# Local and global attention with token routing: global queries scheduled one step earlier, and token ranks from half of the comparisons

## The chip, the cores and the metric

The kernel runs on one core of a Trainium2 chip. A core has five engines, each working through its own queue of instructions in order: PE (TensorE, the matrix unit, whose weight loads are shown as PEld), DVE (VectorE), ACT (ScalarE), POOL (GpSimd) and SP (SyncE, which only issues transfers here). Data lies in the on-chip memory SBUF; matmuls write to the small accumulation memory PSUM, which PE can't read. The engines wait for one another with semaphores.

The metric is device microseconds for one execution. Lower is better.

## The reference

There are 8 batches and 8 heads of width 64, 512 local tokens and 32 global ones.

```python
s_g = scale * q_g @ concat(k_g, k_l).T          # global queries see every key
out_g = softmax(s_g) @ concat(v_g, v_l)
s_ll = scale * q_l @ k_l.T, masked to |i - j| <= 32
s_lg = scale * q_l @ k_g.T                      # local queries see a window and the global keys
out_l = softmax(concat(s_lg, s_ll)) @ concat(v_g, v_l)
x = concat(out_g, out_l) as [8, 544, 512]
scores = x @ w_gate
for b in range(8):                              # the 128 tokens of the highest score
    top = argpartition(-scores[b], 128)[:128]
    y = relu(x[b, top] @ w1) @ w2               # w1 is 512 x 1024, w2 is 1024 x 512
    out[b, top] = x[b, top] + sigmoid(scores[b, top]) * y
```

So every batch needs its attention first, then a choice of 128 of its 544 tokens, then two dense layers on these, which are called the expert work below.

## The kernel before

**Steps.** The attention is cut into 32 steps, the list `work`: for each batch `b`, for each group `hq` of four heads, for each half `hf` of the local tokens. Two steps share one group's queries, keys and values. A group n covers steps 2n and 2n+1. The main loop is a pipeline over three steps. In step i it

- transposes the probabilities of step i (`transp`, L216) into a PSUM tile,
- computes the scores of step i+2 (`scores`, L188) and adds the mask and takes the row maxima on DVE (`maxima`, L201 and L203),
- takes the exponentials of step i+1 on ACT (`exps`, L209, eight instructions),
- copies the transposed tile to SBUF on ACT (`turned`, L221),
- multiplies the probabilities of step i-1 with the values (`attend_mm`, L238) and normalizes them on DVE (`attend_out`, L249 to L256).

**Global queries.** They use the same keys and values of the group. For group n, `g_scores` (L284), the maximum `g_max` (L288) and the exponential `g_exp` (L298) are at the end of step 2n, `g_transp` (L311) and the copy `g_turned` (L316) at the end of step 2n+1, and `g_attend` (L326) and `g_out` (L336 to L345) in step 2n+2. `g_out` stores the result to memory, and for a batch's second group reads all 32 rows back as tile `xg` for their scores.

**PSUM.** `s_tile()` hands out a pool of two buffers (tiles named s_ps). Each step takes three: the transposes, the scores, and the tile `big` of the global queries. The output of attend has one buffer (o_ps), taken anew in each step; the columns behind the local results hold the global result and a small tile of the ranking. The expert work takes its tiles from a third pool of two (m_ps).

**Loads.** `load` fetches q_t, k_t and qg_t of a group, with two buffers each, `load_v` one half of its values, with four buffers. `load` for group n+2 stands at the head of step 2n+1; both halves of the values of group n+1 are asked for in step 2n, behind `g_out`. SP issues all of these and the stores of `finish` and `g_out`. The order on PE, DVE, ACT and POOL is that of the program text (`manual_schedule`, L70); the order on SP is set by a planner.

**Ranks.** When a batch is complete, its tokens' scores are on DVE (`score`, L269, one fused multiply and sum per 128 tokens). Then a generator `chain` takes it through stages, one per step: score of the global rows, `spread` (all 544 scores laid along the free axis of every partition, tile r), `rank` for the five blocks of tokens, `onehot`, `gather`, and a wait of two steps. `rank(b, i)` compares every token of block i with all tokens: one instruction counts those of greater or equal score up to and including its own block (L371), one those of greater score from its own block on (L373); the matrix side_w holds the weights 0 and 1 that break ties by position. A token's rank is the sum of both. `onehot` (L381, L383) compares the ranks with the slot numbers 0 to 127, `gather` turns that into a list of token numbers by five matmuls of one column (L398) and fetches the rows with an indirect transfer (L403). The list `RATE` says how many blocks are ranked per step.

**Expert work.** It is cut into pieces in a list `fill`, each with a cost (1.3 for twelve matmuls of L485 or six of L501), and `run_fill` puts a third of a step's share at three places of each step; the share is at most `FILL` and is worked out from what is left and when it is due. Batches are taken in `GROUPS`. `work` items that are not done by the last step follow it, with the last batch's ranking between them: `GPRE`, `TAKES` and `GPOS` say how many pieces stand ahead of it, behind each block's ranking, and behind the onehot. Functions put into the list `early` run in the next step between attend_mm and attend_out.

## Time and profile before

| | |
|---|---|
| median of three runs | 366.64 us |
| the three runs | 366.64, 362.34, 366.88 us |
| the profiled execution | 365.06 us |
| its span, from first to last instruction | 363.3 us |
| mean granted TensorE clock | 0.921 |
| busy share of PE, DVE, ACT, POOL | 78, 68, 45, 10 % |
| bytes moved | 76.07 MB |

The profile was taken in one execution. Its page gives the busy time of each engine over the span. The trace behind it can be cut into windows (busy time of each engine in each), grouped by source line (busy time, mean duration, and the idle time of the engine ahead of the group), listed by waits (engine, line, what released it: us in total, how often, the longest), followed back from the end as a chain of waits, or read as a timeline. A name such as L188 is the line of the kernel that recorded the instruction; "s_ps<-k_t,q_t" says that it writes tile s_ps and reads k_t and q_t. A wait on "issue" ends on nothing that the profile shows. Matmuls overlap, so a busy PE is not a PE at its peak.

### The profile page before, as it was taken

Reading aid. Unit: us, or ns where it says so; the run is one execution under the profiler, and the core shown is the slowest. Engines: PE = TensorE matmul, PEld = TensorE weight load, DVE = VectorE, ACT = ScalarE, POOL = GpSimd, SP = SyncE. Lnnn points to the kernel's source line nnn. Section 1 sums busy time; section 2 is a strip of 40 time slices with the busy share of each in tenths; the row PEclk is TensorE's granted clock in tenths of the full one; section 3 lists DMA queues with packets and bytes.
Section 4 is the critical chain, followed back from the end, with each engine's and each line's share of the span. In section 5 each row is a group of like instructions: output and inputs, shape, how many; then the busy total and the mean of one; then the engine's idle time right before and its main releaser. Section 6 shows DMA issues by size and latency. Waiting matters only on the chain.

```text
span 363.3 us, 13847 instructions
## 1 busy us (share of the span) xinstructions
PE 283.6 (78%) x6136; PEld 225.8 (62%) x6136; DVE 245.4 (68%) x593; ACT 164.0 (45%) x411; POOL 37.9 (10%) x30
## 2 busy tenths in 40 slices
PE   6768484865496978878779699889788982989994
PEld 3546363654374766756567688667568871779883
DVE  1466555569977896799769867996678769293222
ACT  1644919091738264837454357235644620112020
POOL 1000505040230001001000100010000101111111
PEclk9989969698859899999969999999999996799998
DMA  7995979697849486875867648496770122101000
GB/s 257 416 387 190 346 276 324 220 359 257 278 127 383 165 308 203 320 279 183 284 231 231 241 161 316 135 329 202 287 286 20 23 74 69 39 20 59 31 29 29
DMA packets 22636, 76.07 MB, mean 209 GB/s; under 512 B 6576, under 2 KB 7984, under 8 KB 18480
## 3 DMA queue, kind: packets, MB, share of 16 engines
q1 hardware_dynamic: 21296, 70.99, 54.3%
q0 software_dynamic: 1280, 4.20, 3.6%
q8 instruction: 48, 0.79, 0.9%
q14 instruction: 12, 0.10, 0.1%
HBM read 64.16 MB, written 11.01 MB: 207 GB/s over the span
## 4 chain that ended last, share of the span: by engine, by line
issue 61%; PE 13%; DMA 7%; DVE 7%; POOL 4%; ACT 4%; SPq 1%; POOLq 1%; ACTq 0%; DVEq 0%
DMA k_t<-in_kT_dram 5%; PE s_ps L188 5%; PE o_ps L238 3%; POOL xe L403 2%; POOL out_dram L508 2%; PE o_ps L326 2%; ACT p_t L209 1%; DVE nb L203 1%; DVE p_t L201 1%; DMA qg_t<-in_qgT_dram 1%; PE s_ps L216 1%; DVE x L256 1%; DVE mx L288 1%; ACT pg L298 1%; PE m_ps L457 1%
## 5 line engine op out<-in xcount | busy, mean ns | idle before, releaser
L209 ACT ACTIVATE p_t<-p_t,nb 128x128 f32<-128x128 f32 x256 | 78.2, 394 | 13.0 <-DVE nb L203 8.6
L188 PE MATMUL s_ps<-k_t,q_t 64*32 64x128 f32 x2048 | 44.9, 308 | 37.7 <-ACT pg L298 18.5
L201 DVE SCALAR_TENSOR_TENSOR p_t<-s_ps,cs 128x1024 f32<-128x1024 f32 x32 | 39.1, 1223 | 49.0 <-PE s_ps L188 49.0
L188 PEld LDWEIGHTS s_ps<-k_t,q_t 64*32 64x32 f32 x2048 | 33.6, 117 | 46.7 <-ACT pg L298 21.7
L238 PE MATMUL o_ps<-v_t,pt 128*32 128x65 f32 x2048 | 42.8, 238 | 6.5 <-issue 6.5
L238 PEld LDWEIGHTS o_ps<-v_t,pt 128*32 128x32 f32 x2048 | 36.0, 120 | 15.3 <-issue 13.5
L298 ACT ACTIVATE pg<-s_ps,nbg 128x64 f32<-128x64 f32 (+1 forms) x32 | 13.8, 483 | 69.4 <-DVE nbg L290 57.9
L203 DVE TENSOR_REDUCE nb<-p_t 128x8 f32<-128x1024 f32 x32 | 39.0, 1220 | 1.1
L216 PE MATMUL s_ps<-cs,p_t 128*128 128x128 f32 x256 | 37.1, 291 | 2.9 <-ACT pt L221 1.5
L216 PEld LDWEIGHTS s_ps<-cs,p_t 128*128 128x128 f32 x256 | 30.8, 148 | 6.1 <-ACT pt L221 1.9
L221 ACT COPY pt<-s_ps 128x1024 f32<-128x1024 f32 x32 | 31.9, 996 | 0.5 <-PE s_ps L216 0.5
L371 DVE SCALAR_TENSOR_TENSOR junk<-r,sc,side_w 128x128 f32<-128x128 f32 (+4 forms) x40 | 23.8, 595 | 3.1 <-ACT r L359 1.7
L485 PE MATMUL m_ps<-xTh,w1h 128*128 128x256 f32 x84 | 22.5, 301 | 4.1 <-DVE hTl L488 3.2
L403 POOL DMA_INDIRECT xe<-out_dram,ix x8 | 9.0, 1120 | 152.8 <-DVE ix L401 119.3
L501 PE MATMUL m_ps<-w2h,hTh 128*128 128x512 f32 x56 | 24.9, 444 | 0.0
L269 DVE CUSTOM_DVE_ANT_0 junk<-x,wgb 128x512 f32<-128x512 f32 x32 | 24.2, 757 | 0.8
L373 DVE SCALAR_TENSOR_TENSOR junk<-r,sc,side_w 128x544 f32<-128x544 f32 (+4 forms) x40 | 22.6, 565 | 1.6
L501 PE MATMUL m_ps<-w2l,hTh 128*128 128x512 f32 x56 | 23.1, 412 | 0.0
L256 DVE TENSOR_TENSOR x<-o_ps,rec 128x512 f32<-128x512 f32 x32 | 22.1, 692 | 1.1
L485 PE MATMUL m_ps<-xTh,w1l 128*128 128x256 f32 x84 | 20.7, 279 | 0.0
L284 PE MATMUL s_ps<-k_t,qg_t 64*32 64x512 f32 (+1 forms) x256 | 20.5, 438 | 0.0
L316 ACT COPY ptg<-s_ps 128x768 f32<-128x768 f32 x16 | 12.8, 800 | 14.8 <-PE s_ps L311 14.7
(113 smaller groups left out, 424.8 us busy)
## 6 DMA issues: line engine op xcount, KB each, us to landing
v_t<-in_vw_dram SPq DMA_DIRECT2D x32, 1040.0 KB, 5.9
k_t<-in_kT_dram SPq DMA_DIRECT2D x15, 832.0 KB, 7.9
out_dram<-x SPq DMA_DIRECT2D x32, 256.0 KB, 5.1
q_t<-in_qT_dram SPq DMA_DIRECT2D x15, 512.0 KB, 7.4
ws<-in_w_dram SPq DMA_DIRECT2D x8, 512.0 KB, 7.6
q_t<-in_qT_dram SPq DMA_DIRECT2D x2, 256.0 KB
qg_t<-in_qgT_dram SPq DMA_DIRECT2D x16, 32.0 KB, 5.9
out_dram<-ogs SPq DMA_DIRECT2D x16, 32.0 KB
```

The source lines that it names most:

```text
L188: nc.tensor.matmul(out=s_ps[32 * j:32 * j + 32, par, pr, t, :], lhsT=q_t[rows, pr, 32 * c:32 * c + 32], rhs=window(k_t[rows, pr, k0:k0 + P ...
L201: nc.vector.scalar_tensor_tensor(out=p_t, in0=s_ps.rearrange("p a r t k -> p (a r) t k"), scalar=0.125, in1=m, op0=ALU.mult, op1=ALU.add)
L203: nc.vector.tensor_reduce(out=nb, in_=p_t.rearrange("p q t k -> p (q t) k"), axis=AX.X, op=ALU.max, negate=True)
L209: nc.scalar.activation(out=p_t[:, q, t, :], in_=p_t[:, q, t, :], func=AF.Exp, bias=nb[:, 2 * q + t:2 * q + t + 1])
L216: nc.tensor.transpose(t_ps[:, t, q, :], p_t[:, q, t, :], ident)
L221: nc.scalar.copy(out=pt, in_=t_ps)
L238: nc.tensor.matmul(out=o_ps[32 * j:32 * j + 32, t, h, :], lhsT=pt[:, t, 2 * (h % 2) + h // 2, 32 * j:32 * j + 32], rhs=v_t[:, 4 * t + j, h ...
L256: nc.vector.tensor_tensor(out=xt[b, hf][:, :, 4 * hq:4 * hq + 4, :], in0=o_ps[:, :, :, 0:D], in1=rec.broadcast_to([P, 2, 4, D]), op=ALU.mult)
L269: nc.vector.tensor_tensor_reduce(out=junk[:n, 0:DM], in0=xf, in1=wgb[:n], op0=ALU.mult, op1=ALU.add, scale=1.0, scalar=0.0, accum_out=dst,)
L371: nc.vector.scalar_tensor_tensor(out=junk[:n, 0:hi], in0=r[:n, 0:hi], scalar=s, in1=side_w[:n, P + SL - lo:P + SL - lo + hi], op0=ALU.is_g ...
L485: nc.tensor.matmul(out=h_ps, lhsT=a[:, kc, ms], rhs=xT[x_][:, kc, :], start=(i == 0), stop=(i == len(prods) - 1))
L501: nc.tensor.matmul(out=y_ps, lhsT=hT[h_][:, mc, cc], rhs=w[:, mc, :], start=(part == 0 and i == 0), stop=(part == 3 and i == len(prods) - 1))
```

## The change

- The global queries go one step earlier: `g_scores`, `g_max` and `g_exp` of group n+1 in step 2n+1 (the first group's ahead of the loop), `g_transp` and `g_turned` of group n in step 2n, `g_attend` and `g_out` of group n in step 2n+1. Their tile is filled right behind the scores of step i+2, ahead of the first third of the expert pieces, and is emptied on ACT behind that third.
- `turned` stands ahead of the masks and maxima and of the exponentials.
- `load` of group n+2 stands at the head of step 2n. The values of group n+1 are asked for at the heads of steps 2n and 2n+1, one half each.
- A batch's `chain` begins one step earlier; all five blocks are ranked in one step, and `RATE` is gone.
- Block i is compared only with the tokens from its own block on. The outcomes are kept, as ones and zeros in fp16 (`won`). The sum along a row is the number of later tokens that beat a token, as before. For the earlier tokens, `beaten` lets PE sum the outcomes by column against a column of minus ones, 15 matmuls per batch into the o_ps bank; what is missing to a count of the earlier tokens that win is a constant per token, and it is put into the slot numbers that `onehot` compares with, `slot16`, now one row set per block.
- Some constants and scratch tiles become smaller, the last ranking's takes change.

```diff
-RATE = (3, 2.5, 3, 2.5, 3, 2.5, 3)
-TAKES = (1, 1, 1, 1, 1)
-GPOS = 3
+TAKES = (1, 0, 1, 0, 0)
+GPOS = 1
...
-    side_w = cst.tile([P, SL + 2 * P], FP32, name="side_w")
-    nc.gpsimd.memset(side_w[:, P:P + SL], 1.0)
+    side_w = cst.tile([P, ST], FP16, name="side_w")
+    nc.gpsimd.memset(side_w[:, P:ST], 1.0)
+
+    won = [cst.tile([P, P * (NT + 1 - i)], FP16, name=f"won{i}") for i in range(NT + 1)]
+    for i in range(NT + 1):
+        nc.gpsimd.memset(won[i][:, ST - P * i:], 0.0)
+    nc.gpsimd.memset(won[NT], 0.0)
+    neg1 = cst.tile([P, 1], FP16, name="neg1")
+    nc.vector.memset(neg1, -1.0)
...
-    slot16 = cst.tile([P, NST * P], FP16, name="slot16")
+    slot16 = cst.tile([P, NT + 1, NST * P], FP16, name="slot16")
...
-        junk = moe.tile([P, ST], FP32, name="junk")
+        junk = moe.tile([P, DM], BF16, name="junk")
...
     def rank(b, i):
         r, cnt = rk[b]
         n = P if i < NT else SG
-        s = sc[b][0:n, i:i + 1]
-        lo, hi = P * i, P * i + n
-        junk = moe.tile([P, ST], FP32, name="junk")
-        nc.vector.scalar_tensor_tensor(out=junk[:n, 0:hi], in0=r[:n, 0:hi], scalar=s, in1=side_w[:n, P + SL - lo:P + SL - lo + hi],
-                                       op0=ALU.is_ge, op1=ALU.mult, accum_out=cnt[:n, i, 0:1])
-        nc.vector.scalar_tensor_tensor(out=junk[:n, lo:ST], in0=r[:n, lo:ST], scalar=s, in1=side_w[:n, 0:ST - lo],
-                                       op0=ALU.is_gt, op1=ALU.mult, accum_out=cnt[:n, i, 1:2])
+        lo = P * i
+        nc.vector.scalar_tensor_tensor(
+            out=won[i][:n, 0:ST - lo], in0=r[:n, lo:ST], scalar=sc[b][0:n, i:i + 1], in1=side_w[:n, 0:ST - lo],
+            op0=ALU.is_gt, op1=ALU.mult, accum_out=cnt[:n, i:i + 1])
+
+    def beaten(b):
+        ps = ob["o"][:, 0, 4 * VD + SG:4 * VD + SG + NT + 1]
+        for a in range(NT + 1):
+            for i in range(a + 1):
+                n = P if i < NT else SG
+                nc.tensor.matmul(out=ps[:, a:a + 1], lhsT=won[i][0:n, P * (a - i):P * (a - i) + P], rhs=neg1[0:n],
+                                 start=(i == 0), stop=(i == a), skip_group_check=True)
+        rk[b] = (ps, rk[b][1])
...
     def onehot(b):
-        _, cnt = rk[b]
+        ps, cnt = rk[b]
         rank_t = sm.tile([P, NT + 1], FP16, name="rank")
-        nc.vector.tensor_tensor(out=rank_t, in0=cnt[:, :, 0], in1=cnt[:, :, 1], op=ALU.add)
+        nc.vector.tensor_tensor(out=rank_t, in0=ps, in1=cnt, op=ALU.add)
...
-            out=oh[b], in0=slot16.rearrange("p (a n) -> p a n", a=1).broadcast_to([P, NT + 1, NST * P]),
+            out=oh[b], in0=slot16,
...
-        i = 0
-        acc = 0.0
-        while i <= NT:
...
-        if RATE[b] <= 2:
-            yield
+        for i in range(NT + 1):
+            rank(b, i)
+        early.append((beaten, (b,)))
+        yield
         onehot(b)
...
     load(0, 0)
+    load(0, 1)
     load_v(0, 0, 0)
-    load(0, 1)
     load_v(0, 0, 1)
...
-        nc.sync.dma_start(out=side_w[:, 0:P], in_=const[:, o:o + P])
-        nc.sync.dma_start(out=side_w[:, P + SL:], in_=const[:, o + P:o + 2 * P])
+        tri = wst.tile([P, 1024], FP32, name="ws")
+        nc.sync.dma_start(out=tri[:, 0:P], in_=const[:, o:o + P])
+        nc.gpsimd.tensor_copy(out=side_w[:, 0:P], in_=tri[:, 0:P])
...
     exps(*PR[0])
+    big = s_tile()
+    g_scores(0, 0, big)
+    gst["pg"] = g_exp(big, g_max(big))
     for i in range(nstep + 1):
...
-            if hf == 1 and i // 2 + 2 < B * NQ:
-                load(*divmod(i // 2 + 2, NQ))
+            if hf == 0 and n + 2 < B * NQ:
+                load(*divmod(n + 2, NQ))
+            if n + 1 < B * NQ:
+                load_v(*divmod(n + 1, NQ), hf)
...
         if i + 2 < nstep:
-            PR[i + 2] = maxima(work[i + 2], scores(work[i + 2]))
+            s_ps = scores(work[i + 2])
+        if g is not None:
+            PT[i] = turned(t_ps)
+        if i + 2 < nstep:
+            PR[i + 2] = maxima(work[i + 2], s_ps)
         if i + 1 < nstep:
             exps(*PR[i + 1])
+
+        big = nb = None
+        if g is not None and (hf == 0 or n + 1 < B * NQ):
+            big = s_tile()
+            if hf == 0:
+                g_transp(gst["pg"], big)
+            else:
+                g_scores(*divmod(n + 1, NQ), big)
+                nb = g_max(big)
         if g is not None:
-            PT[i] = turned(t_ps)
             run_fill(part / 3)
+        if big is not None:
+            if hf == 0:
+                gst["ptg"] = g_turned(big)
+            else:
+                gst["pg"] = g_exp(big, nb)
         if i > 0:
             o_ps = attend_mm(work[i - 1], PT.pop(i - 1))
-            if i % 2 == 0:
+            if i % 2:
                 g_attend(*work[i - 1][:2], gst["ptg"])
...
-            if i % 2 == 0:
+            if i % 2:
                 g_out(*work[i - 1][:2])
-
-        if g is not None and hf == 0 and nxt[0] < B:
-            for k in range(2):
-                load_v(*nxt, k)
         if g is not None:
             run_fill(part / 3)
-            big = s_tile()
-            if hf == 0:
-                g_scores(b, hq, big)
-                gst["pg"] = g_exp(big, g_max(big))
-            else:
-                g_transp(gst["pg"], big)
-                gst["ptg"] = g_turned(big)
...
-        if 1 < i < nstep and i // per_b and i % per_b == 1:
+        if 1 < i < nstep and i // per_b and i % per_b == 0:
             chains.append(chain(i // per_b - 1))
...
-            nc.vector.tensor_copy(out=slot16, in_=slot)
+            for a in range(NT + 1):
+                nc.vector.tensor_scalar(out=slot16[:, a], in0=slot, scalar1=tokid[:, a:a + 1],
+                                        scalar2=float(SG if a < NT else -SL), op0=ALU.subtract, op1=ALU.add)
...
         rank(B - 1, i)
         take(TAKES[i])
+    beaten(B - 1)
     onehot(B - 1)
```

18 lines of the change are left out of this document (5 added, 13 removed).

## The prediction

> **What bounds the kernel now.** I read the engine totals of the page first.
>
> ```profile
> span 363.3 us, 13847 instructions
> PE 283.6 (78%) x6136; PEld 225.8 (62%) x6136; DVE 245.4 (68%) x593; ACT 164.0 (45%) x411; POOL 37.9 (10%) x30
> ```
>
> No engine is full over the span, so the limit has to be read by stage. The next view cuts the span at the first local transpose of a step (step 0 at 11.3, step 9 at 88.2, step 31 at 288.6); its columns are busy time of PE, PEld, DVE, ACT, POOL, then PE's granted clock, the DMA share and GB/s.
>
> ```profile
> 11.30:88.20 76.90, 52.05 (x1462) 39.48 (x1462) 45.43 (x87) 43.87 (x108) 14.45 (x6) 0.87 0.84 304
> 88.20:160.00 71.80, 56.29 (x1453) 43.33 (x1445) 58.49 (x135) 38.47 (x95) 7.22 (x4) 0.90 0.72 255
> 160.00:226.00 66.00, 53.74 (x1313) 44.47 (x1311) 52.09 (x130) 35.82 (x95) 3.32 (x3) 0.95 0.69 244
> 226.00:288.60 62.60, 53.96 (x1294) 43.53 (x1293) 50.98 (x131) 31.21 (x82) 3.32 (x4) 0.97 0.53 186
> 288.60:306.80 18.20, 9.71 (x227) 8.56 (x225) 13.13 (x44) 3.87 (x8) 0.59 (x1) 0.88 0.24 80
> 306.80:363.30 56.50, 50.31 (x269) 42.27 (x269) 21.98 (x66) 8.84 (x23) 7.80 (x7) 0.92 0.09 33
> ```
>
> Three stages: nine early steps without expert work (8.5 us each, PE busy two thirds), 22 steps with it (200.4 us, PE busy 164.0, the sum of three rows), and a tail of 74.7 us. The same view cut by head groups (two steps each) shows a second pattern.
>
> ```profile
> 78.13:99.61 21.48, 11.17 (x350) 8.63 (x348) 20.34 (x45) 11.94 (x27) 4.71 (x2) 0.88 0.80 274
> 134.69:151.21 16.52, 13.82 (x365) 10.58 (x364) 11.31 (x25) 9.18 (x24) 1.15 (x1) 1.00 0.80 286
> 151.21:168.99 17.78, 14.32 (x372) 11.15 (x370) 17.04 (x45) 9.61 (x24) 0.00 (x0) 1.00 0.77 267
> ```
>
> A group in which a batch is ranked has DVE full (20.34 of 21.48, 17.04 of 17.78); a group without ranks has DVE at 11.31 of 16.52. So one group of each batch is bound by DVE, the other by what PE waits for. Those waits, for steps 9 to 31, then for the early steps:
>
> ```profile
> PE s_ps L188 <- ACT pg L298: 12.9, 8, 3.5
> PE s_ps L311 <- ACT pt L221: 4.3, 4, 2.0
> PE s_ps L188 <- DMA k_t<-in_kT_dram: 3.5, 3, 2.2
> ...
> PE s_ps L188 <- DMA k_t<-in_kT_dram: 5.6, 2, 4.4
> PE s_ps L188 <- ACT pg L298: 5.5, 4, 1.8
> PE s_ps L188 <- issue: 4.8, 2, 2.8
> ```
>
> The chain of waits shows how the early steps are tied together:
>
> ```profile
> 51.25 2.02 PE s_ps L284 x16
> ...
> 55.24 1.16 PE s_ps L188 x64
> ...
> 57.16 7.56 DMA k_t<-in_kT_dram
> 64.86 1.96 PE s_ps L188 x64
> ```
>
> k_t has two buffers. The global scores (L284) are the last reader of one, ending at 53.3; only then may the keys two groups ahead be fetched, and the fetch goes out at 57.16 and takes 7.56 us, while the scores that need it (L188) stand next on PE. That loop closes once per group.
>
> **The change, part by part.** The sum is made against the profiled execution, 365.06 us (span 363.3 plus 1.8 around it); the median of the three runs, 366.64, lies 1.6 above it.
>
> *Global queries one step ahead.* g_scores of group n moves from step 2n to step 2n-1, right behind the local scores; g_transp to 2n, g_attend and g_out to 2n+1. The last read of k_t then comes a step earlier, and `load` moves from the head of the odd step to that of the even one, so the 7.56 us have about two steps more, some 17 us. The k_t waits go: 5.6 and 3.5. The two v_t loads are split over two steps; both value halves still have over a step. On SP the loads now stand at other places among the stores of finish, the ogs store and the xg read, which waits for that store; SP's order is not fixed by the program text but by the planner (rival 1).
>
> The global tile sits in the same two-buffer pool as the scores. Today it is emptied at the end of a step, and the next L188 waits for the exp (L298): 5.5 and 12.9 us. Now it is emptied in mid-step, behind which a third of the filling, attend and two more thirds follow on PE, so I let both numbers go. In exchange PE meets the global tile right behind L188 and needs the local copy `turned` (L221) done; everything else of the step is queued behind that wait. The change puts the copy ahead of the eight exps on ACT, where it stood behind them, and L188 covers it:
>
> ```profile
> L221 ACT COPY pt<-s_ps x32: 984/995/1014, 15.6 to 289.8; 128x1024 f32<-128x1024 f32 x32
> L371 DVE SCALAR_TENSOR_TENSOR junk<-r,sc,side_w 128x128 f32<-128x128 f32 (+4 forms) x40 | 23.8, 595 | 3.1 <-ACT r L359 1.7
> L371 DVE DVE_READ_ACCUMULATOR junk<-r,sc,side_w 128x1 f32 x32 | 2.7, 83 | 0.0
> L373 DVE SCALAR_TENSOR_TENSOR junk<-r,sc,side_w 128x544 f32<-128x544 f32 (+4 forms) x40 | 22.6, 565 | 1.6
> L398 PEld LDWEIGHTS <-oh x40: 90/96/116, 98.5 to 326.9; 128*128 128x128 f16 x32, 32*128 32x128 f16 x8
> 306.81 0.38 PE L398 MATMUL s_ps<-tok,oh 128*128 128x1 f16 x5 [8.50 <-DVE oh L383]
> ```
>
> 0.995 us against the 1.16 of L188: nothing is left to wait, and the L311 wait on that copy (4.3) goes too. Without this cover the copy would cost up to 1 us per step (rival 3).
>
> *Half the comparisons.* L371 goes, with its accumulator reads: (23.8 + 2.7) / 8 = 3.3 us of DVE per batch; the five of L373 stay, 22.6 / 8 = 2.8 and five reads of 0.08. Their output becomes fp16 while one input stays fp32; I expect the duration of now (bounds: 0 to half less). In the ranked groups this takes DVE from 17.04 to 13.7 of 17.78, so DVE no longer stands in the way when PE's waits go: without it the gain from the global shift would end at DVE's 17.
>
> *Counting on PE.* `beaten` adds 15 matmuls of one column per batch. Nearest row: five of the same shape in L398 take 0.38. Three times that is 1.1, and the pipeline's fill counts once instead of three times, so I take 0.9, by the row of the same shape in sequence; upper bound 15 loads of 0.096 end to end, 1.4; lower 0.7. The Trainium skill, "TensorE: Matmul & The Clock Gate", section "LDWEIGHTS (loading the stationary operand)", speaks against the change: a load costs its columns, here 128, at 1.2 GHz, an estimate of 107 ns and 1.6 us per batch. By it the sum would be some 5 us higher over eight batches; the trace's five in 0.38 do not agree with it. `beaten` is queued ahead of attend_out, so DVE's den waits 0.9 longer in one step of four, where DVE has room now. It writes into the o_ps bank, of which there is one: the next attend waits for the onehot's read in the step before; that read stands a third of a step ahead of it on DVE, so I cost it at nothing, and at about 1.5 us (two scores, L269 below) once per batch if DVE lags.
>
> *Order of the chain.* Each batch's chain starts one step earlier and ranks in one step. By the program's credits (costs 1.3 per piece), 9.1 units are left after the steps before and 6.5 after: two ffn2 pieces leave the tail.
>
> *Small things.* Three const loads become two, slot16 is written by five small operations instead of one, POOL gets some memsets and a copy: DVE has 31 us free in the early stage and POOL is 10% busy, so nothing; uncovered they cost 1 to 2 us once.
>
> Rows for the sums, of the expert matmuls just after the tail's gap and when warm, of DVE's groups, and of the gather's transfer (us to landing):
>
> ```profile
> 307.71 0.63 PE L501 MATMUL m_ps<-w2l,hTh 128*128 128x512 f32 x1
> 308.14 0.63 PE L501 MATMUL m_ps<-w2h,hTh 128*128 128x512 f32 x1
> ...
> 313.94 0.40 PE L501 MATMUL m_ps<-w2h,hTh 128*128 128x512 f32 x1
> 314.17 0.39 PE L501 MATMUL m_ps<-w2l,hTh 128*128 128x512 f32 x1
> L256 DVE TENSOR_TENSOR x<-o_ps,rec 128x512 f32<-128x512 f32 x32 | 22.1, 692 | 1.1
> L269 DVE CUSTOM_DVE_ANT_0 junk<-x,wgb 128x512 f32<-128x512 f32 x32 | 24.2, 757 | 0.8
> L383 DVE TENSOR_TENSOR oh<-slot,rank 128x640 f16<-128x640 f16 x8 | 6.6, 826 | 0.3
> xe<-out_dram,ix POOLq DMA_INDIRECT x8, 3.5
> ```
>
> **Sums by stage.** Early: waits that go 5.6 + 5.5 = 11.1. The floor is DMA: 304 GB/s over 76.9 us are 23.4 MB, and a saturated stretch is seen:
>
> ```profile
> 11.30:28.35 17.05, 11.65 (x231) 8.42 (x232) 8.13 (x11) 9.41 (x27) 0.00 (x0) 0.90 1.02 402
> ```
>
> At 402 GB/s the stage takes 58.2. I take -10 (350 GB/s, about midway); bounds 0, if a share of 0.84 is all it gives, and -18.7. Steps 9 to 31: 12.9 + 4.3 + 3.5 = 20.7 go; PE gets 6 x 0.9 of beaten and the two pieces. Those are twelve matmuls of L501 at the warm pitch of 0.23 us, 2.8. So -12.5; bounds -3 (new waits take the place) and -18 (PE, 164.0 + 8.2, busy to 94%).
>
> The tail: PE idles 8.5 us for batch 6's onehot (L398 above), and the twelve matmuls after it start every 0.43 instead of 0.23. After the change that onehot lies in step 31, but the gather's index still stands on DVE behind two attend_outs (0.69 of L256 and two small operations, about 1.1 each), g_out (about 0.6), onehot (0.83 and a small one, 1.0) and four scores (0.757 each): 7 us, then 3.5 to landing, and PE has only some 5.8 us of work ahead of it (beaten, two ffn2 pieces, attend, gather, one expand). So I expect 5 us of idle in place of 8.5, and half of the slow stretch's 2.4 back. The Trainium skill, "TensorE: Matmul & The Clock Gate", section "Part 1: The HAM clock gate", says that an idle window of about 3.4 us halves the clock; the trace agrees (L188 takes 1.96 behind the k_t wait of 4.4, and 1.16 otherwise), and by that rule all of the 2.4 stays and the sum is 1.2 higher. Two pieces leave: -2.8. Batch 7: beaten +0.9, and only two pieces cover 3.2 us of ranks, one free operation covers the onehot: about +2.4 idle, bounds 0 and 5. Tail: -3.5 - 1.2 - 2.8 + 0.9 + 2.4 = -4 (bounds -9 and +2).
>
> Start: the first group's global scores, max and exp come before step 0 (up to the 2.02 of L284), while the second group's keys are now asked for ahead of the values, for a gain that no row prices. I take 0, and 2 either way for the range.
>
> Sum: -10 - 12.5 - 4 = -26.5, 338 us. Its own range, from the bounds taken half together: 326 to 350.
>
> **Rivals.** Two per cent, about 7.3 us, is what a measurement of this kernel tells from no change.
> 1. *SP's queue eats the head start*: the planner leaves loads behind the xg read and stores. Early gain then only the 5.5 less a quarter for the denser queue, -4; steps -8; tail -4: 349. For it: the 4 us between 53.3 and 57.16. Against: a whole step of new slack. Chance 0.15.
> 2. *Refills*: PE's waits that end on "issue" (4.8 on L188 early) grow when loads are denser; the gain halves, 352, or vanishes with PE bound anyway, 362. Chance 0.15.
> 3. *Slower*: PE stuck at the global tile, because ACT reaches the copy late behind the exp that waits for DVE's maximum. Each of 31 steps costs w; the 26.5 are used up at w = 0.85, two per cent are lost from 1.1. With 2 us, the longest L311 wait, in two steps of three: 338 + 41 = 379. Against: 0.995 under 1.16. Chance 0.05.
> 4. *Better*: early at 402 GB/s, steps at the bound, tail -9: -45, 320. Chance 0.12.
> 5. The forecast: 0.53.
>
> Faster: 0.53 + 0.12 + 0.15 + 0.05 of rival 2; same 0.10; slower 0.05. The range leaves out rival 3, the 362 of rival 2 and the edge of rival 4: 322 to 356.
>
> **What would show it.** Right: no k_t or L298 wait left on L188; L373's successor at 2.8 us per batch; ranked groups with DVE near 14; early steps near 7.4 us; the idle before the last-but-one gather near 5. Wrong: PE waiting for L221's copy at the global tile in most steps; the DMA share above 0.95 early with PE waiting on issue; beaten above 1.4 us; early stage unchanged at 76.9.

## The result, and the profile after

| | before | after |
|---|---|---|
| median | 364.49 us of 4 runs (361.14 to 366.88) | 346.60 us of 4 runs (345.10 to 347.62) |
| profiled execution | 365.06 us, span 363.3 | 346.12 us, span 344.3 |
| ratio | | 0.9558, interval 0.9492 to 0.9624 |

The change saves 17.9 us, and 18.9 between the two profiled executions, where 26.5 were forecast. The ratio leaves out executions more than 1.5% above the fastest of their kernel, so it isn't the quotient of the two medians. A further six runs of the changed kernel, in the last experiment below, had a median of 347.87 us and a ratio of 0.957 (0.9505 to 0.9635); the ten together have a median of 347.1.

The engine totals of the changed kernel, in the columns of the page:

```profile
span 344.3 us, 14004 instructions
PE 288.6 (84%) x6256; PEld 229.8 (67%) x6256; DVE 217.0 (63%) x518; ACT 165.3 (48%) x411; POOL 38.5 (11%) x37
```

DVE lost 28.4 us of work, and PE gained 5.0. The span cut at the same places as before (first local transposes of steps 0, 9 and 31, now L222), with the busy time of PE, PEld, DVE, ACT and POOL, PE's granted clock, the DMA share and GB/s:

```profile
12.13:83.57 71.44, 52.29 (x1479) 39.45 (x1472) 47.10 (x97) 43.10 (x104) 14.94 (x7) 0.86 0.85 320
83.57:275.71 192.14, 171.94 (x4152) 138.75 (x4152) 138.56 (x332) 108.33 (x274) 14.41 (x11) 0.96 0.70 242
275.71:344.30 68.59, 56.18 (x484) 47.28 (x482) 27.17 (x85) 9.96 (x24) 7.26 (x7) 0.94 0.13 45
```

Each stage splits into PE's busy time and the rest, in which PE is idle. The three rows of before for the steps add up to 164.0 busy of 200.4; its tail is this row:

```profile
288.60:363.30 74.70, 60.01 (x496) 50.83 (x494) 35.12 (x109) 12.72 (x31) 8.40 (x8) 0.91 0.13 45
```

| stage | PE idle before, after | PE busy before, after | sum of both changes | forecast |
|---|---|---|---|---|
| start | | | +0.8 | 0 |
| steps 0 to 9 | 24.9, 19.2 | 52.1, 52.3 | -5.5 | -10 |
| steps 9 to 31 | 36.4, 20.2 | 164.0, 171.9 | -8.3 | -12.5 |
| tail | 14.7, 12.4 | 60.0, 56.2 | -6.1 | -4 |

What PE waits for now, over the whole span (engine, line, releaser: us in total, times, longest), and what ACT waits for on transfers:

```profile
PE s_ps L290 <- DVE p_t L207: 8.7, 4, 3.3
PE o_ps L332 <- issue: 7.7, 5, 2.4
PE s_ps L317 <- ACT pt L227: 5.1, 4, 2.5
PE s_ps L439 <- DMA xe<-out_dram,ix: 4.3, 1, 4.3
...
PE s_ps L194 <- DMA k_t<-in_kT_dram: 2.7, 2, 1.9
PE s_ps L194 <- ACT pg L304: 2.5, 3, 1.8
```

```profile
ACT w1h L159 <- DMA ws<-in_w_dram: 15.1, 3, 8.6
ACT w2h L159 <- DMA ws<-in_w_dram: 14.4, 3, 7.6
```

The two waits at the local scores (now L194) that the prediction wanted to remove are nearly gone: the keys cost 2.7 us, the global exponential 2.5. But two others stand near the head. L290, the global scores, had no such wait before; L317, the global transposes, waited 4.3 us for the local copy before (as L311) and now waits 5.1. Together they wait 13.8 us. L317 waits for the local copy. L290 waits for DVE's first operation on the local scores (L207, the mask). The timeline shows one such place, in step 3 (start, duration, engine, line; in brackets the idle time ahead):

```profile
33.31 1.23 DVE L207 SCALAR_TENSOR_TENSOR p_t<-s_ps,cs 128x1024 f32<-128x1024 f32 x1 [0.58 <-PE s_ps L194]
34.59 1.12 PE L290 MATMUL s_ps<-k_t,qg_t 64*32 64x512 f32 x16 [1.40 <-DVE p_t L207]
39.48 1.04 ACT L159 CAST w1h<-ws 128x1024 fp32r<-128x1024 f32 x1 [8.57 <-DMA ws<-in_w_dram]
40.43 1.00 ACT L227 COPY pt<-s_ps 128x1024 f32<-128x1024 f32 x1
```

PE resumes 0.05 us after L207 ends, and 5.8 us ahead of the step's copy (L227). So the tile that L290 fills here is not that of the transposes, which the copy has yet to empty, but that of the local scores computed right ahead of it. The same rows show what is new on ACT: the copy stands 8.57 us behind a split of expert weights (L159) that waits for its transfer. Such waits add up to 29.5 us; the prediction did not speak of them.

Four of the sixteen global tiles are filled like this, in steps 3, 5, 7 and 9 of both traces of the changed kernel: PE starts them some 0.05 us after the mask ends. Most of the others start as closely behind the local copy. In step 7 (3.28 us) the mask itself stands behind the five comparisons of a batch, which run from 67.61 to 69.80.

By stage, the first nine steps and then steps 9 to 31 (the same view):

```profile
PE s_ps L290 <- DVE p_t L207: 6.8, 3, 3.3
...
PE s_ps L317 <- ACT pt L227: 1.8, 2, 1.1
```

```profile
PE s_ps L317 <- ACT pt L227: 3.3, 2, 2.5
...
PE s_ps L290 <- DVE p_t L207: 1.9, 1, 1.9
```

In the first nine steps 11.1 us of waits for the keys and the exponential have become 11.1 us of other ones: 6.8 and 1.8 at the global tile, and all of the 2.5 for the exponential. That PE's idle time fell there all the same is in its waits on "issue": 11.5 us before, 5.7 now. In steps 9 to 31, 5.2 us have come in the place of 20.7.

The comparisons on DVE (busy, mean ns, idle ahead), two places of PE's timeline in the tail, and two neighbouring groups of steps, in the first of which a batch is ranked:

```profile
L376 DVE SCALAR_TENSOR_TENSOR won<-r,sc,side_w 128x544 f16<-128x544 f32 (+4 forms) x40 | 18.1, 512 | 1.9 <-ACT r L368 1.9
```

```profile
279.82 0.61 PE L386 MATMUL o_ps<-neg,won 128*128 128x1 f16 x15
...
291.52 1.01 PE L439 MATMUL s_ps<-cs,xe 128*128 128x128 f32 x4 [4.33 <-DMA xe<-out_dram,ix]
```

```profile
128.59:145.16 16.57, 16.49 (x385) 13.11 (x385) 12.00 (x32) 10.61 (x26) 0.00 (x0) 0.92 0.64 218
145.16:162.26 17.10, 12.87 (x361) 10.19 (x359) 13.39 (x30) 8.36 (x22) 1.20 (x1) 1.00 0.85 285
```

A batch's comparisons keep DVE busy for 18.1 / 8 = 2.3 us and its accumulator reads for 0.4, and its counting (`beaten`, L386) takes 0.61 us. With the chain one step earlier, a batch's comparisons (here from 137.62 on) and its onehot no longer fall into one group: DVE is busy 12.00 of 16.57 in the first and 13.39 of 17.10 in the second. Over all groups that hold a batch's comparisons it is busy 57 to 89%, where such groups had it at 79 to 96% before.

### The profile page after: what moved, and what is told of

Its sections match the earlier page's. It is cut to its first block, busy times and chain, and to the rows that moved or that the text cites. A ratio compares the mean times of both kernels' runs of the same rounds, so it can differ in the third digit from the quotient of the medians.

```text
span 344.3 us, 14004 instructions
## 1 busy us (share of the span) xinstructions
PE 288.6 (84%) x6256; PEld 229.8 (67%) x6256; DVE 217.0 (63%) x518; ACT 165.3 (48%) x411; POOL 38.5 (11%) x37
## 4 chain that ended last, share of the span: by engine, by line
issue 50%; PE 23%; DMA 10%; DVE 6%; ACT 4%; POOL 3%; SPq 1%; POOLq 1%; ACTq 0%; DVEq 0%
DMA ws<-in_w_dram 5%; PE s_ps L194 5%; PE o_ps L244 4%; DMA k_t<-in_kT_dram 4%; PE s_ps L222 3%; PE s_ps L290 2%; PE s_ps L317 2%; POOL out_dram L523 2%; PE m_ps L472 2%; PE o_ps L332 2%; POOL xe L418 2%; DVE p_t L207 1%; ACT pt L227 1%; ACT p_t L215 1%; DVE x L262 1%
## 5 line engine op out<-in xcount | busy, mean ns | idle before, releaser
L207 DVE SCALAR_TENSOR_TENSOR p_t<-s_ps,cs 128x1024 f32<-128x1024 f32 x32 | 39.0, 1218 | 34.8 <-PE s_ps L194 29.3
L194 PE MATMUL s_ps<-k_t,q_t 64*32 64x128 f32 x2048 | 44.8, 294 | 9.3 <-issue 4.1
L227 ACT COPY pt<-s_ps 128x1024 f32<-128x1024 f32 x32 | 32.4, 1012 | 31.4 <-PE s_ps L222 31.4
L194 PEld LDWEIGHTS s_ps<-k_t,q_t 64*32 64x32 f32 x2048 | 32.4, 113 | 19.3 <-issue 15.1
L244 PE MATMUL o_ps<-v_t,pt 128*32 128x65 f32 x2048 | 40.1, 233 | 4.5 <-issue 2.7
L222 PE MATMUL s_ps<-cs,p_t 128*128 128x128 f32 x256 | 40.2, 297 | 3.5 <-ACT p_t L215 3.5
L244 PEld LDWEIGHTS o_ps<-v_t,pt 128*32 128x32 f32 x2048 | 34.2, 117 | 10.8 <-issue 8.3
L222 PEld LDWEIGHTS s_ps<-cs,p_t 128*128 128x128 f32 x256 | 31.9, 150 | 9.2 <-ACT p_t L215 6.2
L255 DVE TENSOR_SCALAR den<-o_ps 128x8 f32<-128x8 f32 x32 | 5.3, 164 | 35.6 <-ACT r L368 14.0
L290 PE MATMUL s_ps<-k_t,qg_t 64*32 64x512 f32 (+1 forms) x256 | 20.0, 425 | 8.9 <-DVE p_t L207 8.7
L275 DVE CUSTOM_DVE_ANT_0 junk<-x,wgb 128x512 bf16<-128x512 f32 x32 | 23.6, 738 | 0.8
L332 PE MATMUL o_ps<-v_t,ptg 128*32 128x65 f32 x768 | 17.2, 232 | 7.7 <-issue 7.7
L290 PEld LDWEIGHTS s_ps<-k_t,qg_t 64*32 64x32 f32 x256 | 8.5, 113 | 22.1 <-issue 10.0
L304 ACT ACTIVATE pg<-s_ps,nbg 128x64 f32<-128x64 f32 (+1 forms) x32 | 13.8, 481 | 17.7 <-DVE nbg L296 16.5
L317 PE MATMUL s_ps<-cs,pg 128*128 128x128 f32 x96 | 16.1, 309 | 5.3 <-ACT pt L227 5.1
```

The source lines that it names most:

```text
L194: nc.tensor.matmul(out=s_ps[32 * j:32 * j + 32, par, pr, t, :], lhsT=q_t[rows, pr, 32 * c:32 * c + 32], rhs=window(k_t[rows, pr, k0:k0 + P ...
L207: nc.vector.scalar_tensor_tensor(out=p_t, in0=s_ps.rearrange("p a r t k -> p (a r) t k"), scalar=0.125, in1=m, op0=ALU.mult, op1=ALU.add)
L222: nc.tensor.transpose(t_ps[:, t, q, :], p_t[:, q, t, :], ident)
L227: nc.scalar.copy(out=pt, in_=t_ps)
L244: nc.tensor.matmul(out=o_ps[32 * j:32 * j + 32, t, h, :], lhsT=pt[:, t, 2 * (h % 2) + h // 2, 32 * j:32 * j + 32], rhs=v_t[:, 4 * t + j, h ...
L275: nc.vector.tensor_tensor_reduce(out=junk[:n], in0=xf, in1=wgb[:n], op0=ALU.mult, op1=ALU.add, scale=1.0, scalar=0.0, accum_out=dst,)
```

## The experiments

**Theory and rivals at the start.** The theory: the two halves of the change each do what the prediction said and the missing 7.6 us (26.5 less the 18.9 between the profiled executions) are ACT's new wait for the weights, which delays the copy and so PE. Rivals: the gain is one half's alone; the missing time is in the waits that took the place of the old ones at the global tile; or in PE's waits on "issue".

### The weights are split one step later

```diff
-        if wl:
+        if len(wl) > 1 or (wl and i >= WSTART + 8):
             split(*wl.pop(0))
```

> The changed kernel with one edit: the split of an expert weight tile on ACT stands one step behind its load instead of at the end of the same step. In the changed kernel ACT waits 29.5 us for these loads (15.1 for w1, 14.4 for w2), ahead of the copy L227 that the global tile on PE needs. Theory, that this wait is what holds the early steps: it is nearly gone, the early stage (71.4 us) falls by 6 to 9 and the time to about 338 to 340. Rival, that the early steps are held by the bytes (342 to 351 GB/s in half of them): the wait turns up at q_t, k_t or v_t, and the time stays within 2 us of 346.6.

Measured: 351.25 us (349.26 to 353.07), ratio 0.9728 (0.964 to 0.9816). The weight waits are off ACT and the kernel became no faster: by the medians it is 4 to 5 us slower. So that ACT waits for weights costs nothing that this edit gives back; the theory fell, and its rival, which expected no change, was off too. PE's waits at the global tile stayed, on the other line (L317 for the mask, 7.0 us in the first nine steps). In the profiled execution steps 9 to 31 (192.7 us) and the tail (68.4) are those of the changed kernel; what is longer is steps 0 to 9, at 77.0 us, a stage that two traces of the changed kernel have at 71.4 and 79.8 (last run below).

### The new order alone, with the old ranking

All ten comparisons of a batch, as before the change, in one step; their constants and scratch tiles go back with them. The order, the early loads and the takes are those of the change.

```diff
     def rank(b, i):
...
-        nc.vector.scalar_tensor_tensor(
-            out=won[i][:n, 0:ST - lo], in0=r[:n, lo:ST], ...
+        nc.vector.scalar_tensor_tensor(out=junk[:n, 0:hi], in0=r[:n, 0:hi], ...
+        nc.vector.scalar_tensor_tensor(out=junk[:n, lo:ST], in0=r[:n, lo:ST], ...
...
-        early.append((beaten, (b,)))
         yield
         onehot(b)
```

> The changed order with the full ranking of before (ten comparisons per batch, no counting on PE), all else as in the changed kernel. Theory of the prediction, that ranked groups meet DVE once PE's waits are gone: DVE gets 3.4 us more in each of six or seven ranked groups that have it at about 13 of 17, and the time is 8 to 15 us above the changed kernel, 355 to 361. Rival, that PE is the bound there (90% busy after step 9): only the tail's ranking shows, +2 to +4 less the 0.6 of counting per batch, 346 to 350.

Measured: 371.72 us (370.27 to 373.3), ratio 1.0297 (1.0216 to 1.0377): slower than the kernel before, where both theories expected a gain. The twenty-first step, in which a batch is ranked, of this kernel and then of the changed one, and what PE waits for longest in this kernel's:

```profile
189.61:206.24 16.63, 10.82 (x180) 9.68 (x179) 13.52 (x37) 5.44 (x14) 0.00 (x0) 0.79 0.39 137
```

```profile
177.11:187.00 9.89, 9.84 (x195) 8.98 (x194) 8.31 (x23) 5.41 (x13) 0.00 (x0) 0.90 0.51 177
```

```profile
PE m_ps L484 <- DVE xTl L427: 5.0, 1, 5.0
```

The step takes 6.74 us more, the largest difference of any step from 9 to 31, and PE stands 5.0 us for an operand of the expert work (xTl) that DVE makes behind the comparisons. Of the 5.21 us that DVE has more to do in it, 3.7 are the ranking (192.88 to 198.84, in place of 178.41 to 180.69); the rest are operations that the changed kernel has done when the step begins.

### The same, ranked over two steps

```diff
         for i in range(NT + 1):
+            if i == 3:
+                yield
             rank(b, i)
-        yield
         onehot(b)
```

> The changed order with the full ranking, as in the run with all ten comparisons in one step (371.7), but three blocks ranked in one step and two in the next, ahead of the onehot. Theory, that the run of ten comparisons blocks DVE's queue for 6 us, with the expert work's subtraction and then PE behind it: 358 to 364. Rival, that the total of DVE's work is what costs: within 3 us of 371.7.

Measured: 371.84 us (370.34 to 375.38), ratio 1.0305. Spreading the work over two steps changed nothing, as the rival said. So the amount of DVE's work, and not that it comes in one burst, is what the new order can't bear, as far as this one way of spreading shows. The wait moves to the global tile:

```profile
PE s_ps L283 <- DVE p_t L200: 12.7, 4, 4.8
```

### The new ranking alone, in the old order

The main loop, the loads, the chains' start and the takes of before, with `won`, `beaten` and `slot16` of the change; all five blocks are ranked in one step, as in the change.

```diff
-        if g is not None and (hf == 0 or n + 1 < B * NQ):
-            big = s_tile()
-            if hf == 0:
-                g_transp(gst["pg"], big)
...
         if g is not None:
             run_fill(part / 3)
+            big = s_tile()
+            if hf == 0:
+                g_scores(b, hq, big)
+                gst["pg"] = g_exp(big, g_max(big))
```

> The kernel before with the new ranking alone (five comparisons kept, counted on PE), global queries, loads and chain starts where they were. Theory, that a ranked group was bound by DVE: about 3 us per batch in six groups and the tail, 15 to 20 below before, 345 to 350. Rival, that the waits for k_t and for the global exp hold the groups whatever DVE does: 3 to 6 below before, 359 to 362.

Measured: 356.08 us (351.95 to 358.0), ratio 0.9889 (0.9821 to 0.9957), between the two forecasts. The waits that the order is to remove are all there:

```profile
PE s_ps L195 <- DMA k_t<-in_kT_dram: 14.2, 9, 2.8
PE s_ps L195 <- ACT pg L305: 13.2, 9, 2.7
```

So the halves don't add up. Against the median of before on the same occasion (362.24 us), the ranking alone gives -6.2 (about -4 by the ratio) and the order alone +9.5, which is +3.3; both together gave -17.9. Steps 9 to 31 show the same by themselves, with the order alone and then the ranking alone (before 200.4 us, both 192.1):

```profile
91.03:296.45 205.42, 166.84 (x4076) 134.13 (x4076) 156.73 (x387) 106.87 (x273) 14.63 (x11) 0.94 0.63 223
```

```profile
83.57:279.26 195.69, 162.41 (x4130) 131.91 (x4121) 140.25 (x336) 105.17 (x270) 14.04 (x11) 0.97 0.65 235
```

The order costs 5.0 us there (4.1 when ranked over two steps), the ranking gives 4.7, and both together give 8.3. The order pays only once DVE has been relieved.

### The loads at their old places

```diff
-            if hf == 0 and n + 2 < B * NQ:
+            if hf == 1 and n + 2 < B * NQ:
                 load(*divmod(n + 2, NQ))
-            if n + 1 < B * NQ:
-                load_v(*divmod(n + 1, NQ), hf)
...
+        if g is not None and hf == 0 and n + 1 < B * NQ:
+            for k in range(2):
+                load_v(*divmod(n + 1, NQ), k)
```

> The changed kernel with the loads at their old places in the text: queries and keys at the head of the odd step, both halves of the values behind g_out in the even step. Theory, that the early load call is needed to end the k_t waits: the waits of L194 for k_t come back in part, +3 to +8, 350 to 354. Rival, that freeing the key buffer a step earlier is enough, and that SP's planner orders the loads by itself: within 2 us of the changed kernel; it could even be faster by 2 to 4, since the expert weights then stand ahead of the keys.

Measured: 348.67 us (345.14 to 349.95), ratio 0.968 (0.9622 to 0.9739). The wait for the keys is back in full, as the theory said, at 16.3 us over the span. The time rose by 2.1 us only by the medians, less than the spread of the runs, and by some 4 us by the ratios:

```profile
PE s_ps L194 <- DMA k_t<-in_kT_dram: 16.3, 5, 6.3
```

A wait that is 13.6 us longer cost 2 to 4. The waits at the global tile are 4.0 us in this trace, in place of 13.8: where the one wait goes, another takes its place. That the keys come earlier is worth little by itself.

### No values fetched after the first two groups

The values of the first batch's two groups serve for all batches, so the outputs are made of other values; 28 of the 32 transfers of 1,040 KB are left out.

```diff
     def load_v(b, hq, half):
+        if NQ * b + hq >= 2:
+            loaded[b, hq][3].append(loaded[0, hq][3][half])
+            return
         v_t = vld.tile([P, 8, 4, VD], FP32, name="v_t")
```

> The changed kernel with the values fetched for the first two groups only; all later groups use those tiles (so their outputs are of other values; every instruction of the engines stays). This takes 29 of 76 MB from the queue. Theory, that PE's waits inside a run of matmuls (13.0 us in the changed kernel, 28.1 with the split one step later, nearly all 256 instructions apart or a multiple of it) are refills of its instructions standing behind data transfers, and that the rest of the early loss is ACT waiting for expert weights behind the same transfers: these waits fall under 4 us, ACT's waits for the weights from 29.5 to under 8, and the time to 328 to 334. Rival, that the waits are of PE's own pace: still 10 to 16 us of them, and 340 to 345.

Measured: 330.81 us (328.65 to 334.92), ratio 0.9119 (0.9038 to 0.9201). The time is what the theory said, but not by the way that it gave: PE's waits at steps of 256 instructions fell to 8.8 us and ACT's waits for weights to 11.7, where it had them under 4 and under 8. The first nine steps, in the profiled execution (334.92 us, the longest of the four):

```profile
11.10:83.90 72.80, 50.58 (x1471) 38.85 (x1471) 50.11 (x95) 46.19 (x110) 14.80 (x8) 0.85 0.68 243
```

They are no shorter at a DMA share of 0.68 than the 71.4 us of the changed kernel's first trace at 0.85. What they moved, 243 GB/s over 72.8 us or 17.7 MB, would take 44 us at the 402 GB/s from which the prediction made the floor of this stage, so in this run at least the transfers' rate is far from what held it. PE's longest wait in them, 7.4 us at the global scores, is for a copy that stands behind ACT's wait for weights. The gain is in steps 9 to 31 (180.7 us, against 192.1). Most of it, 9.2 us, lies in the seven steps from 9 to 16; two runs below come near to that with all transfers in place, so not all of it is the transfers' own.

### Three pieces between the last gather and its use

In the tail the expansion of the last-but-one batch (L439) stands first in the list of pieces, right behind its gather. Here three pieces go ahead of it.

```diff
         k = 0 if all(...) else len(fill)
+        if end["on"] and k == 0 and len(tiles) == 2:
+            k = min(3, len(fill))
         fill[k:k] = first
```

> The changed kernel with the two transposes of the last pair group standing behind three waiting pieces (two of them ffn2 matmuls) instead of ahead of them in the tail. Theory, that the tail's 4.3 us of PE idle for batch 6's gathered rows is bare: most of it is covered, the tail falls by 2 to 3.5, the time to 343 to 345. Rival, that the pieces are missing as cover for the last batch's ranking: its idle grows by as much, and the time stays within 1 us of the changed kernel.

Measured: 345.11 us (341.5 to 348.56), ratio 0.9496 (0.9377 to 0.9615). The tail fell from 68.6 us (66.9 in the second trace of the changed kernel, below) to 64.1, by about as much as the wait that it hides:

```profile
278.43:342.50 64.07, 54.84 (x484) 45.97 (x482) 27.17 (x85) 9.90 (x24) 7.45 (x7) 0.95 0.13 48
```

The median lies 1.5 to 2.0 us lower only (346.6 or 347.1 to 345.11); the earlier stages of this execution were 2.7 us longer.

### The global tile behind attend

```diff
-        big = nb = None
+        if g is not None:
+            run_fill(part / 3)
+        if i > 0:
+            o_ps = attend_mm(work[i - 1], PT.pop(i - 1))
...
             if hf == 0:
                 g_transp(gst["pg"], big)
+                gst["ptg_next"] = g_turned(big)
             else:
                 g_scores(*divmod(n + 1, NQ), big)
-                nb = g_max(big)
-        if g is not None:
-            run_fill(part / 3)
...
-        if i > 0:
-            o_ps = attend_mm(work[i - 1], PT.pop(i - 1))
-            if i % 2:
-                g_attend(*work[i - 1][:2], gst["ptg"])
+                gst["pg"] = g_exp(big, g_max(big))
+        if i > 0 and i % 2:
+            g_attend(*work[i - 1][:2], gst["ptg"])
+        if g is not None and hf == 0:
+            gst["ptg"] = gst["ptg_next"]
```

> The changed kernel with the global tile (its scores or transposes, its maximum, exponential and copy) moved on PE from right behind the local scores to behind the first third of the expert pieces and attend_mm, ahead of g_attend; nothing is left out. Theory: the waits that took the place of those forecast to vanish are a matter of cover. PE reaches the global tile so soon behind the local scores that neither DVE (8.7 us, L290 behind the maxima) nor ACT's copy (5.1 us, L317) is done; with a third of the pieces and attend_mm between, both together fall from 13.8 to under 6 us, and the time goes to 337-341. Rival: the loss only moves on; the global tile is now emptied later, the local scores of the next step stand right behind it, and their wait for the global exponential grows from 2.5 to 10 us or more, as before the change (18.5): 345-350.

Measured: 344.99 us (341.4 to 349.91), ratio 0.9503 (0.9418 to 0.9587). The waits did as the theory said, 13.8 to 4.5 us, and the wait for the global exponential grew to 4.5 only:

```profile
PE s_ps L290 <- DVE p_t L207: 3.7, 2, 3.2
...
PE s_ps L317 <- ACT pt L227: 0.8, 1, 0.8
```

The median is at the edge of the rival's range, the profiled execution (341.4) at that of the theory. So 9.3 us fewer of these waits came with some 2 us by the median. In the first nine steps, where 8.6 of the 13.8 had lain, nothing was gained (71.1 us against 71.4). Steps 9 to 31 took 188.1 us in place of 192.1 (193.0 and 193.7 in two more traces that have these steps unaltered), and the gain is in the first seven of them, 56.3 us in place of 61.6 (60.8 in the second trace of the changed kernel, below):

```profile
82.93:139.23 56.30, 48.67 (x1321) 37.19 (x1321) 41.95 (x101) 35.08 (x86) 6.84 (x4) 0.97 0.88 312
```

Against the second trace, at the same granted clock of 0.97, the gain is in PE's idle time (7.6 us in place of 11.5). Against the first, with its clock of 0.89, it is in the busy time (48.7 us in place of 53.4). What these waits had cost is therefore not shown beyond some 2 to 4 us.

### The two edits together

The diffs of the two sections above, in one kernel.

> The edit of the run before this one (global tile behind attend_mm) and that of e8_expand_behind (three pieces ahead of the last-but-one expert batch in the tail) together; nothing is left out. If the first gives what its theory says, the two lie in different stages (steps and tail) and add up: tail near 64, steps near 188, 334-338. If it gives nothing, the time is that of the second alone, 343-347.

Measured: 343.61 us (337.49 to 345.75), ratio 0.9484 (0.9411 to 0.9558). The median is what was expected if the first edit gives nothing; the profiled execution, the fastest of the four at 337.49, is what was expected if both add up. Its tail:

```profile
271.04:335.70 64.66, 54.95 (x484) 46.37 (x482) 27.29 (x85) 9.85 (x24) 7.56 (x7) 0.96 0.13 48
```

Its steps 9 to 31 took 184.3 us (the seven from 9 on 53.8) and its tail 64.7, while its first nine steps took 75.7. It is the fastest kernel here that computes the whole result, by 3.5 us against the ten runs of the changed kernel; the intervals of the ratios overlap, so it is likely the better one, and not shown to be.

### Where the steps of 256 instructions fall

PE's waits on "issue" inside a run of matmuls nearly all come at multiples of 256 recorded instructions of PE. In the changed kernel they add up to 13.0 us, in the run with the later split to 28.1. Two runs move all of them by 32 matmuls of one column:

```diff
         nc.tensor.matmul(out=w_ps, lhsT=wz[:, 0:P], rhs=wz, start=True, stop=True)
+    for i in range(32):
+        nc.tensor.matmul(out=w_ps[:, i:i + 1], lhsT=wz[:, 0:P], rhs=wz[:, 0:1], start=True, stop=True)
```

> The changed kernel with 32 matmuls of one column added to the warming-up at the start, under the first loads: PE's later instructions stand 64 places further, so that refills fall at other matmuls. Theory, that where a refill falls decides whether it meets a queue of data: the waits at 256-instruction steps change from 13.0 us by 4 or more either way, and the time by 2 to 6 with them. Rival: 13.0 and the time stay within 2 us.

Measured: 349.48 us (345.79 to 353.51), ratio 0.9621 (0.9526 to 0.9716), and 19.2 us of such waits. And the same with the later split:

> e1_split_later with 32 one-column matmuls added to the warm-up, as in e9_shift; nothing is left out. e1 had 28.1 us of waits of PE at steps of 256 instructions where the changed kernel has 13.0. If its loss of 4.7 us lies in where these steps fall among the instructions, moving them by 32 changes their sum by 5 us or more (to under 23) and the time to 343-348. If it lies in the later split itself, by PE and DVE work that it delays, both stay: 26-31 us of such waits and 350-354.

Measured: 350.24 us (346.45 to 354.75), and 24.3 us of such waits. The waits fell between the two forecasts. The median is the rival's, but two of the four runs, 346.45 and 347.81, are the theory's and at the level of the changed kernel, so the time decides nothing. By the first run alone the place of the steps would seem to decide. The control is the unaltered kernel, traced again:

> The changed kernel itself, unaltered, traced a second time; nothing is left out. It tells how far one trace may be trusted for PE's waits at steps of 256 instructions (13.0 us in the first trace, 19.2 with 32 instructions more, 28.1 and 24.3 with the split later). If the place of these steps among the instructions decides, the second trace has them at the same instructions and 11-15 us in all. If they fall by chance, with what the transfers happen to do, places and total differ: by 4 us or more, and then the differences between the variants (6.2, 3.8) are not shown to come from the place. The time, 344-348, is to hold either way.

Measured: 347.87 us (345.67 to 352.71), with 18.4 us of such waits. The profiled execution took 352.71 us, the longest of the six:

```profile
11.16:90.97 79.81, 55.53 (x1471) 41.50 (x1472) 47.25 (x95) 45.47 (x109) 14.47 (x7) 0.81 0.78 289
90.97:283.96 192.99, 170.05 (x4150) 137.40 (x4151) 140.01 (x334) 107.86 (x273) 14.49 (x11) 0.96 0.69 242
283.96:350.90 66.94, 54.63 (x484) 45.64 (x482) 27.16 (x85) 9.98 (x24) 7.27 (x7) 0.96 0.13 46
```

Six of the waits stand at the same instructions in both traces, with other lengths (0.81 and 2.96 us at one of them), and the totals differ by 5.4. So the 6.2 us between the shifted kernel and the first trace show nothing. Whether the later split costs its 4 to 5 us by itself stays open: its second build doesn't show the cost clear of the scatter.

This trace has a second lesson: the first nine steps took 71.4 us in one execution and 79.8 in the other, of the same kernel. A third trace that has these steps unaltered, that of the three pieces in the tail, has 72.7, so the 79.8 of the longest execution is the exception. Steps 9 to 31 (192.1, 193.0 and 193.7) and the tail (68.6 and 66.9) come out nearly alike. But the shifted kernel, whose steps are unaltered too, took 197.3 us for steps 9 to 31, in the longest of its runs. What one trace says of a stage is known to one or two us at best, to 5 if the execution is a long one, and to 8 in the early stage.

## Why the prediction was right, and where it was not

The forecast was 338 us with a range of 322 to 356, faster at 0.85. It came out faster, and 8.6 us short of the gain. Of the 18.9 us between the profiled executions, the 8.3 of steps 9 to 31 and the 6.1 of the tail come again in the second trace (7.4 and 7.8); the 5.5 of the first nine steps do not (2.9 us longer than before). By its own steps:

**DVE in the ranked groups: right in size, not by group.** The prediction has DVE at about 13.7 us in a ranked group and overlooks that its own earlier chain takes the comparisons out of the group that holds the batch's onehot. Over the two groups of the batch DVE was busy 28.4 us before (11.31 and 17.04, the prediction's rows) and 25.4 now (12.00 and 13.39): 3.0 less, where 3.3 were to go. The comparisons keep DVE busy for 2.3 us per batch where the prediction took 2.8. Half of the difference is one execution of before beside POOL, 2.36 us in place of 0.39 (last section), which raised the mean that it took; the mean is now 512 ns in place of 565. The other half is that they now overlap by 0.07 us each. The fp16 output itself did not change the duration: the widest form takes 778 ns, and 785 before.

**Counting on PE: right in kind, cheaper than taken.** 0.61 us against 0.9. The 1.6 us that the Trainium skill's rule for a load gave ("TensorE: Matmul & The Clock Gate", section "LDWEIGHTS (loading the stationary operand)") is not borne out: 15 loads and matmuls of 128 fp16 columns pass in 0.61 us, 41 ns each. The same page's section "Weight-path perf modes — Fast Weight Load (FWL) and DoubleRow" says that loads of 128 columns that are not FP32 take about half; an estimate from the two is 0.8 us, nearer to the row.

**"Nothing is left to wait": this step failed.** The waits on L188 for the keys and the exponential went, or nearly so, but 13.8 us stand at the global tile (15.4 in the second trace: 12.9 at L290 and 2.5 at L317), where the prediction had nothing. Two things had been overlooked. The global scores can be given the buffer of the local scores just computed, and then PE depends on DVE's first operation on these, 1.23 us long and behind whatever DVE still has queued (in step 7, a batch's comparisons). And the cover compared durations, not when the covered copy can start: on ACT it may stand behind a split of weights. Rival 3 named the place, with ACT alone and at three times the waits that came about (41 us). The run with the tile behind attend shows where the waits come from: with cover between, the two fell to 4.5 us, and to 4.0 with both edits. It doesn't show that they are the missing gain, since it gave back some 2 us by the median.

**The two halves as separate terms: wrong.** The sum let the order's gain stand on its own, with DVE's relief only as a limit that "no longer stands in the way". The order alone is 9.5 us slower than before, the ranking alone 6.2 faster. In steps 9 to 31 alone these are +5.0 and -4.7, and both together -8.3. PE in the new order meets DVE's result in mid-step, so that ranking ahead of it can be on PE's path: with 3.7 us more of it, one step became 6.74 us longer. Halving the comparisons is thus what makes the order pay.

**Steps 9 to 31: -8.3 in place of -12.5, by the idle term.** PE's busy time rose by 7.9 us (6.1 in the second trace), where 8.2 had been added. That this agrees is in part luck: at 0.61 us, the counting of the five batches in this stage and the two pieces account for some 5.9. Its idle time fell by 16.2 (13.5 in the second trace), where 20.7 had been let go; the new waits of 5.2 us at the global tile are about that difference. So the mis-sized term that decides this stage is the waits.

**Early: -10 is not shown, and the -5.5 of the first trace is luck in part.** The 11.1 us of waits that were to go were replaced by as many (11.2 in the second trace). What fell are the waits on "issue", 11.5 us before and 5.7 and 8.2 in the two traces of after, which the sum didn't hold. The stage took 71.4 us in one and 79.8 in the other, against 76.9 in the one trace of before and 73.4 in the run with the ranking alone, in the old order. The floor by transfers was not the bound: without most values, the stage still took 72.8 us at 243 GB/s. What sets it stays open. ACT's wait for the weights is seen to hold PE in single steps, and the run that removed it gained nothing.

**The tail: -6.1 in place of -4.** The idle ahead of the last-but-one gather's rows is 4.33 us, where about 5 was forecast; it is the transfer that ends it (L439), as was said. The next matmuls of the expert work run at the slow pitch again, six of them instead of twelve, which is the half that the prediction gave back:

```profile
292.75 0.63 PE L516 MATMUL m_ps<-w2l,hTh 128*128 128x512 f32 x1
293.18 0.63 PE L516 MATMUL m_ps<-w2h,hTh 128*128 128x512 f32 x1
```

Their starts are 0.43 us apart, and 0.23 from 296.03 on. The rule of the Trainium skill on an idle window ("TensorE: Matmul & The Clock Gate", section "Part 1: The HAM clock gate") holds here, after 4.33 us as after 8.5. That all of the 2.4 us would stay, as the prediction worked out beside it, did not come about. Two terms on the o_ps bank and the last batch changed places: the wait of attend for the onehot's read of that bank, costed at nothing with 1.5 as its bound, took 1.72, and the last batch's onehot 1.12 of the 2.4 taken for it.

```profile
283.74 0.96 PE L244 MATMUL o_ps<-v_t,pt 128*32 128x65 f32 x53 [1.72 <-DVE rank L396]
```

In all PE's idle time fell by 2.3 us where 1.1 was forecast, and its work by 3.8 where the sum had 3.1 (27 matmuls fewer beside `beaten`, for 24).

**Rivals.** Rival 1 (SP's queue eats the head start) did not happen: the wait for the keys went to 2.7 us, and putting the loads back brought it to 16.3. Rival 2 (refills): PE's waits at the 256-instruction steps are 13.0 and 18.4 us in the two traces of after, 10.0 in the one of before. They may have taken a part of the gain; the scatter is as large as the difference. Rival 4 (the early steps at 402 GB/s) did not come about: they ran at 320 and 289.

## What to carry to other kernels

An operation that is moved to a place where it meets another engine's result in mid-step needs the slack of that engine's whole queue, not just a duration that covers it; see which buffer the pool will hand out there, and who empties it. Two edits of which one shifts load to the place that the other relieves are not two terms of a sum: price each alone, and expect that the one that shifts the load may lose without the other. A wait that is gone from a list is a gain only if no other has come in its place: add up the idle time of the stage. And trace the same kernel twice before a difference of a stage is read as the effect of an edit: one stage here repeated within 1 us and another only within 8.

## What had not been expected of the hardware

**PE stops at steps of 256 instructions.** Its waits on "issue" of over 0.2 us inside runs of matmuls fall 256 recorded instructions apart or at multiples of that, up to 4 us each, 9 to 28 us per execution in the kernels here. A few others lie elsewhere, in the kernel before three of 2.0 to 2.8 us. The queue that the page calls "instruction" moves as many packets as PE has such steps:

```profile
q8 instruction: 49, 0.80, 0.9%
```

49 packets of 0.80 MB are 16 KB each, and PE's 12,609 recorded instructions are 49.3 times 256. The Trainium skill, "Runtime: NRT & Kernel Launch", section "Instruction fetch mechanics", tells of blocks of 16 KiB with 256 instructions and calls the cost mostly hidden; here they add up to 13.0 us and more. The least of it, 8.8 us, was seen in the run without most values, whose transfers are fewer; that their number decides is not shown.

**DVE stands still beside POOL.** While POOL subtracts the weights, a DVE operation with two inputs from SBUF that starts meanwhile ends only after it. In the changed kernel, and in the kernel before:

```profile
40.60 2.34 POOL L160 TENSOR_TENSOR w1l<-ws,w1h 128x1024 fp32r<-128x1024 f32 x1 [15.48 <-ACT w1h L159]
...
41.23 2.27 DVE L275 CUSTOM_DVE_ANT_0 junk<-x,wgb 128x512 bf16<-128x512 f32 x1
```

```profile
93.70 2.36 POOL L154 TENSOR_TENSOR w2l<-ws,w2h 128x1024 fp32r<-128x1024 f32 x1 [11.14 <-ACT w2h L153]
...
93.88 2.36 DVE L373 SCALAR_TENSOR_TENSOR junk<-r,sc,side_w 128x160 f32<-128x160 f32 x1
```

The score takes 2.27 us in place of the 0.69 of the next one, the comparison 2.36 in place of 0.39. In the run with the later split, the widest comparison took 2.89 in place of 0.78 (107.38, beside POOL from 107.32). They end 0.56, 0.18 and 0.58 us after POOL does, as though most of their work had waited for it. The mask, of whose two inputs one lies in PSUM, took its usual 1.23 us beside POOL (46.72, POOL from 45.54 to 47.91). The Trainium skill, "SBUF — State Buffer", section "Who interferes with whom", says the two engines share a pair of ports under an exclusive lock; the trace agrees. Where POOL's eight subtractions fall among DVE's work is thus worth up to 2.2 us each on a DVE that PE waits for. Counted as the time beyond the usual duration of such an operation, DVE lost 9.1 and 8.6 us in this way in the two builds of the later split, and 1.6 and 3.2 in the two traces of the changed kernel. That may be what the later split lost, if it lost anything; it was not tried by itself.
